# Cosine attention and a low-rank mixer: batch 0's first loads in halves of the heads

## The chip, the cores and the metric

The kernel runs on one core of a Trainium2 chip. Its time is device microseconds of that core, the median of five runs. The engines are TensorE (PE, with its weight loads as PEld), VectorE (DVE), ScalarE (ACT), GpSimd (POOL) and SyncE (SP), which issues most of the DMAs. Each works through its own instructions in order and waits for others by semaphores.

## What is computed

```python
def phi(x, c, s):                       # c, s: cos and sin of pi/2 * position / S
    r = np.maximum(x, 0.0)
    return np.concatenate([r * c, r * s], axis=-1)
q_p, k_p = phi(q, cos_w, sin_w), phi(k, cos_w, sin_w)
kv  = np.einsum('bhsf,bhsd->bhfd', k_p, v)
z   = np.sum(k_p, axis=2)
num = np.einsum('bhsf,bhfd->bhsd', q_p, kv)
den = np.einsum('bhsf,bhf->bhs', q_p, z)[..., None] + 1e-06
x   = (num / den).transpose(0, 2, 1, 3).reshape(B, S, H * D)

h = x.transpose(0, 2, 1) @ U @ V        # mixes positions, rank 32
u = x + h.transpose(0, 2, 1)
out = u + np.maximum(u @ w_ch1, 0.0) @ w_ch2
```

There are 8 batches of 8 heads, 576 positions, 64 columns a head (512 in all), rank 32, and 2048 hidden columns. Inputs and output are float32.

## The kernel before

All 8 batches are processed on the one core. The 576 positions of a batch are five chunks: position 4p + c for p = 0 to 127 is chunk c (0 to 3), and the last 64 positions are the "tail", chunk 4. So q, k and v each come as a main load (`load_main`, 1 MB or half of it, L74) and a tail load (`load_tail`, 128 KB, L80), all issued on SP. The staging buffers of q and v exist once, those of k twice.

The stages of a batch: `q_prep` and `k_prep` (L251, L257) make relu times cosine and relu times sine in bf16, one instruction for each on ScalarE (L237) or VectorE (L239); `v_prep` and `v_block` (L217, L228) cast v, and put a column of ones beside it; `qtr_unit` (L284) transposes q on TensorE with a copy out of PSUM; `kv_unit` (L263) makes kv and z of four heads; `den_unit` (L325) and `recip` the reciprocals of the denominators; `xh_unit` (L341) the normalised x of four heads and one chunk. `A_unit` (L385) is x times U, with an evacuation for each half of the columns; `V_four` and `V_evac` (L196, L207) expand V for all partitions once; `uTd_open`, `uTd_mm` and `uTd_evac` make u transposed for one of four column blocks d, directly in PSUM. `g1_main` (L483) is one of 16 column blocks of the first channel product, four matmuls over d, and its relu goes to ScalarE (L502); `g2_part` (L527) is the second product.

The order on every engine is written out by hand. From L706 on come warm-up matmuls on zeros (`keep_warm`, L176), batch 0's q and k preparation, then `chain_head(0)` and `chain_mid(0)`, and then the first `g1_main`, of which three are opened with two matmuls each because uT of d 0 and 1 is ready first. After that, a list of slots (L775) gives TensorE's dense work, 16 `g1_main` for each batch of a pair, and other work is put beside numbered slots (`at`, `beside`, `PLAN`). Batch 1's preparation lies beside slots 0 to 6, its chain beside slot 7.

Batch 0's loads are issued in the order q, q tail, k, k tail, v tail, v's heads 0 to 3, v's heads 4 to 7, V, U. Then come batch 1's (L722 to L730). U and V are staged in float32 and cast on GpSimd (`cast_uv`, L185). GpSimd also issues the loads of w_ch1, in four quarters that are cast on the way (`w1_load`, L89). It holds the first quarter back by a one-column copy of batch 0's k tail (`mark`, L717), which waits until that tail has landed; the second stands in the middle of `cast_uv`; the third and the fourth wait for batch 1's q tail copy (L755).

Of the kernel before, what the change touches and what calls it, by code (L numbers as in the profile page):

```python
# [10 lines left out]
FP32 = mybir.dt.float32  # L11
BF16 = mybir.dt.bfloat16
# [5 lines left out]
def kernel(  # L18
# [11 lines left out]
    nc = tc.nc  # L30
# [49 lines left out]
    def load_tail(dst, src, b, eng=None):  # L80
        (eng or nc.sync).dma_start(
            out=dst[tail(b), :, :],
            in_=src[b, :, 512:S, :].rearrange("h s d -> s h d"),
        )
# [24 lines left out]
    st_uv = pool.tile([P, 1024], FP32, tag="hid_tl", bufs=1, name="st_uv")  # L109
    stV = st_uv[0:R, 0:S]  # L110
    stU = st_uv[:, S : S + 5 * R].rearrange("p (c r) -> p c r", r=R)

# [8 lines left out]
    for lo in (0, TS):  # L121
# [4 lines left out]
    load_main(qst[0], q, 0)  # L126
    load_tail(qt[0], q, 0)
    load_main(kst[0], k, 0)
    load_tail(kt[0], k, 0)
    load_tail(vt[0], v, 0)  # L130
    load_main(vst[0], v, 0, 0, 4)
    load_main(vst[0], v, 0, 4, 8)
    nc.sync.dma_start(out=stV, in_=moe_V)
    nc.sync.dma_start(
        out=stU[:, 0:4, :], in_=moe_U[0:512, :].rearrange("(p c) r -> p c r", c=4)
    )
    for lo in (0, TS):
        nc.sync.dma_start(out=stU[lo : lo + TS, 4, :], in_=moe_U[512:S, :])
# [23 lines left out]
    V_32 = const.tile([R, 5, P], BF16)  # L162
    V_bf = const.tile([P, 5, P], BF16)
    four = const.tile([R, 4, R], BF16)
    for g in range(4):
        G_.tensor_copy(out=four[:, g, :], in_=ident[0:R, 0:R])
# [14 lines left out]
    V_.memset(U_bf, 0.0)  # L181
    mark = const.tile([TS, 1], FP32)
    mark2 = const.tile([1, 1], FP32)

    def cast_uv():  # L185
        cast(G_, V_32[:, 0:4, :], stV[:, 0:512].rearrange("r (p c) -> r c p", c=4))
        for i in range(2):
            cast(G_, V_32[:, 4, tail(i)], stV[:, 512:S])
        w1_load(1)
        cast(G_, U_bf[:, 0:4, :], stU[:, 0:4, :])  # L190
        for i in range(2):
            cast(G_, U_bf[tail(i), 4 + i, :], stU[tail(i), 4, :])
# [3 lines left out]
    def V_four(tag, bufs):  # L196
        v4 = v4_ps[0] = ps.tile([P, 2, 512], FP32, tag=tag, bufs=bufs, name="v4_ps")
        lhs = four.rearrange("r g s -> r (g s)")
        nc.tensor.matmul(
            out=v4[:, 0, :], lhsT=lhs, rhs=V_32[:, 0:4, :].rearrange("r c t -> r (c t)"),  # L200
            start=True, stop=True,
        )
        nc.tensor.matmul(
            out=v4[:, 1, 0:P], lhsT=lhs, rhs=V_32[:, 4, :], start=True, stop=True
        )
# [135 lines left out]
    def xh_unit(b, c, h0, h1, rec, tag, bufs):  # L341
        x_alloc(b)
        n = h1 - h0
        rows = slice(0, P) if c < 4 else tail(b)
        acc = ps.tile([P, n, D], FP32, tag=tag, bufs=bufs, name="xh_ps")
        for h in range(h0, h1):
            nc.tensor.matmul(  # L347
                out=acc[:, h - h0, :], lhsT=qT_of(b, c, h), rhs=kv_sb[b][:, h, 0:D],
                start=True, stop=True,
            )  # L350
        nc.vector.tensor_tensor(
            out=x_of(b, c, rows)[:, h0 * D : h1 * D].rearrange("p (i d) -> p i d", d=D),
            in0=acc[rows],
            in1=rec[rows, c, :].unsqueeze(2).to_broadcast([P if c < 4 else TS, n, D]),
            op=ALU.mult,
        )
# [214 lines left out]
    def loads(b, eng):  # L571
        def kk():
            alloc_k(b)
            load_tail(kt[b], k, b, eng)
            load_main(kst[b], k, b, eng=eng)

        def vv():
            alloc_v(b)
            load_tail(vt[b], v, b, eng)
            load_main(vst[b], v, b, eng=eng)  # L580

        def qq():
            alloc_q(b)
            load_tail(qt[b], q, b, eng)
            load_main(qst[b], q, b, eng=eng)

        return kk, vv, qq
# [61 lines left out]
    def chain_head(b, fill, xt):  # L649
        if b == 0:  # L650
            v_prep(b, 0, 4, (4,), (A_,))
            v_block(b, 0, 4, 0, 3, V_)
            v_block(b, 0, 4, 3, 4, A_)
        kv_unit(b, 0, "T", 1)
        fill(0)
        rec0 = den_unit(b, 0, 4, "X", 1)
        if b == 0:
            v_prep(b, 4, 8, (4,), (A_,))
        v_block(b, 4, 8, 0, 4, A_)
        fill(1)  # L660
        for n, c in enumerate(ORD):
            xh_unit(b, c, 0, 4, rec0, *xt[n])
            if n == 1:
                fill(2)
            if n == 3:
                kv_unit(b, 1, "T", 1, A_)
        if b == 0:
            V_four("X", 1)
            V_evac(A_)

    def chain_mid(b, fill, xt, dt):
        fill(3)
        m = 3 if b == 0 else 2
        rec1 = den_unit(b, 4, 8, *dt)
        if b == 1:

            nc.sync.dma_start(out=mark2, in_=rec1[0:1, 0, 0:1])
        for n, c in enumerate(ORD[:m]):
            xh_unit(b, c, 4, 8, rec1, *xt[n])
        u01 = ps.tile([P, 2, 512], FP32, tag="X", bufs=1, name="u01")  # L680
        uTd_open(b, 0, None, None, u01[:, 0, :].rearrange("p (c t) -> p c t", c=4))
        uTd_open(b, 1, None, None, u01[:, 1, :].rearrange("p (c t) -> p c t", c=4))
        a0 = A_unit(b, "T", 1, A_, 0, 256)
        for n in (m, m + 1):
            xh_unit(b, ORD[n], 4, 8, rec1, *xt[n])
        fill(4)
        uTd_mm(b, 0)
        uTd_mm(b, 1)
        uTd_evac(b, 0, A_)
        uTd_evac(b, 1, V_ if b == 0 else A_)  # L690
        for n in range(m + 2, 5):
            xh_unit(b, ORD[n], 4, 8, rec1, *xt[n])
        fill(5)
        return a0
# [6 lines left out]
    def warm0(n):  # L701
        m = (2, 1, 0, 1, 1, 2)[n]
        if m:
            keep_warm(m, *(O2 if n == 0 else G3))

    keep_warm(18, "X", 1)  # L706
    for c in TL:
        q_prep(0, c, (V_, V_ if c == 3 else A_))
    for n, c in enumerate(TL):
        qtr_unit(0, c, 0, H, (V_, A_, V_, A_, V_)[n], *(G3 if n < 3 else O2))  # L710
        if n in (1, 3):
            keep_warm(1, "X", 1)
    for c in TL:
        k_prep(0, c, (V_, V_ if c == 3 else A_))
    keep_warm(13, "o", 2)

    G_.tensor_copy(out=mark, in_=kt[0][0:TS, 0, 0:1])  # L717
    w1_load(0)
    cast_uv()
    chain_head(0, warm0, (O2, O2, G3, G3, O2))  # L720
# [10 lines left out]
    a0 = chain_mid(0, warm0, (O2, G3, O2, G3, O2), G3)  # L731
    for c in (0, 1):
        q_prep(1, c, (None, A_))
# [7 lines left out]
    q_prep(1, 0, (V_, None))  # L741
# [7 lines left out]
    for n, c in enumerate(ORD):  # L749
        if n > 1:  # L750
            at(n - 2, lambda c=c, n=n: q_prep(1, c, (V_, (None, A_, V_)[n - 2])))
# [8 lines left out]
    st1 = {}  # L760

# [6 lines left out]
    xt1 = (O2, O2, O2, O2, O2)  # L768
    at(7, lambda: keep_warm(2, "X", 1))
    at(7, lambda: chain_head(1, fill1, xt1))  # L770
    at(7, lambda: st1.update(a=chain_mid(1, fill1, xt1, ("T", 1))))
    at(7, lambda: chain_end(1, st1["a"]))
# [62 lines left out]
```

## Time and profile before

| | us |
|---|---|
| median of 5 runs (319.48 to 321.08) | 320.46 |
| the profiled execution | 320.94 |
| its span, first to last instruction | 319.0 |
| TensorE busy in it | 308.7 |
| first channel product starts | 23.89 |
| batch 1's q tail is on TensorE | 27.21 |
| batch 1's kv starts | 34.63 |

The profile is of one execution. Times in it count from the span's start; the execution's own time has 1.94 us around the span. A row of the timeline has start, duration, engine, line, operation, output and inputs, shape, count, and in brackets how long the engine was idle before it and who ended that. A helper such as `cast` has one line for all its uses, so tiles tell more than lines. The clock granted to TensorE is 1.00 throughout; matmuls of 512 columns follow each other at 0.43 us until 6.2 us, and at 0.22 us from then on.

### The profile page before, as it was taken

Reading aid. Unit: us, or ns where it says so; the run is one execution under the profiler, and the core shown is the slowest. Engines: PE = TensorE matmul, PEld = TensorE weight load, DVE = VectorE, ACT = ScalarE, POOL = GpSimd, SP = SyncE. Lnnn points to the kernel's source line nnn. Section 1 sums busy time; section 2 is a strip of 40 time slices with the busy share of each in tenths; the row PEclk is TensorE's granted clock in tenths of the full one; section 3 lists DMA queues with packets and bytes.
Section 4 is the critical chain, followed back from the end, with each engine's and each line's share of the span. In section 5 each row is a group of like instructions: output and inputs, shape, how many; then the busy total and the mean of one; then the engine's idle time right before and its main releaser. Section 6 shows DMA issues by size and latency. Waiting matters only on the chain.

```text
span 319.0 us, 5754 instructions
## 1 busy us (share of the span) xinstructions
PE 308.7 (97%) x2359; PEld 162.5 (51%) x2386; DVE 154.0 (48%) x341; ACT 150.6 (47%) x251; POOL 35.0 (11%) x71
## 2 busy tenths in 40 slices
PE   8699899999999999999999999999999999999996
PEld 3465464475545544475455444564454444464443
DVE  5767653762877645036926585154836520001211
ACT  3847756685905256658400077559400166650000
POOL 2132500300120140000221100000121100000000
PEclk9999999999999999999999999999999999999999
DMA  7999999999196937990899659930692140001122
GB/s 224 274 284 212 224 206 281 269 277 262 50 202 160 303 90 142 225 276 10 170 206 317 232 121 179 309 104 30 128 214 73 60 91 0 2 0 68 66 83 81
DMA packets 83755, 51.90 MB, mean 163 GB/s; under 512 B 51890, under 2 KB 80946, under 8 KB 83730
## 3 DMA queue, kind: packets, MB, share of 16 engines
q1 hardware_dynamic: 77154, 40.21, 53.4%
q0 software_dynamic: 6432, 11.27, 14.7%
q8 instruction: 18, 0.29, 0.4%
q10 hardware_dynamic: 144, 0.07, 0.1%
q14 instruction: 7, 0.06, 0.1%
HBM read 36.86 MB, written 9.44 MB: 145 GB/s over the span
## 4 chain that ended last, share of the span: by engine, by line
PE 88%; DMA 7%; ACT 3%; DVE 1%; issue 1%; SPq 0%; DVEq 0%; ACTq 0%
PE o_ps L545 39%; PE g_ps L493 33%; PE gt_ps L513 4%; DMA qt<-in_q_dram 4%; DMA kst<-in_k_dram 3%; PE kv_ps L271 3%; PE x_ps L365 3%; PE va_ps L409 3%; ACT k_p L237 1%; PE t_ps L288 1%; PE a_ps L392 1%; ACT hid L502 1%; PE d_ps L330 0%; PE xh_ps L347 0%; ACT k_tl L237 0%
## 5 line engine op out<-in xcount | busy, mean ns | idle before, releaser
L502 ACT ACTIVATE hid<-g_ps 128x512 bf16<-128x512 f32 x128 | 76.2, 596 | 100.0 <-PE g_ps L493 99.4
L493 PE MATMUL g_ps<-uT,w_bf 128*128 128x512 bf16 x512 | 118.5, 379 | 0.2
L545 PE MATMUL o_ps<-w_bf,hid 128*128 128x512 bf16 (+2 forms) x510 | 117.3, 372 | 1.0
L493 PEld LDWEIGHTS <-w_bf 128*128 128x128 bf16 x512 | 48.8, 98 | 55.9 <-issue 0.4
L545 PEld LDWEIGHTS <-hid 128*128 128x128 bf16 x528 | 48.7, 98 | 52.8 <-issue 1.7
L555 DVE TENSOR_TENSOR o_sb<-u_bf,o_ps 128x512 f32<-128x512 bf16 (+2 forms) x33 | 22.1, 668 | 62.7 <-PE o_ps L545 62.6
L565 POOL DMA_DIRECT2D out_dram<-o_sb x24 | 13.5, 562 | 162.9 <-DVE o_sb L555 152.9
L410 DVE TENSOR_TENSOR u_bf<-x_bf,va_ps 128x512 bf16<-128x512 bf16 x32 | 21.8, 685 | 10.2 <-PE va_ps L409 9.7
L105 DVE CAST kv<-kv_ps 128x260 bf16<-128x260 f32 x14 | 6.0, 429 | 32.7 <-PE kv_ps L271 32.7
L237 ACT ACTIVATE q_p<-qst,sinw 128x512 bf16<-128x512 f32 x22 | 15.1, 711 | 4.3 <-DMA qst<-in_q_dram 4.2
L375 DVE TENSOR_TENSOR x_bf<-x_ps,rec 128x512 bf16<-128x512 f32 x24 | 16.6, 691 | 0.8
L513 PE MATMUL gt_ps<-uT_tl,w_bf 128*128 128x128 bf16 x256 | 15.6, 219 | 0.0
L513 PEld LDWEIGHTS <-w_bf 128*128 128x128 bf16 x256 | 14.6, 98 | 0.5
L545 PE MATMUL o_ps<-w_bf,hid_tl 128*128 128x512 bf16 x61 | 14.6, 379 | 0.2
L271 PE MATMUL kv_ps<-v_ext,k_p 128*128 128x65 bf16 x256 | 12.1, 193 | 2.7 <-DVE v_ext L105 1.8
L322 DVE TENSOR_SCALAR rec<-x_ps 128x8 f32<-128x8 f32 (+1 forms) x30 | 4.9, 165 | 20.2 <-PE x_ps L365 20.2
L271 PEld LDWEIGHTS <-k_p 128*128 128x128 bf16 x256 | 11.3, 97 | 6.4 <-ACT v_ext L103 2.0
L409 PE MATMUL va_ps<-A_sb,V_bf 128*128 128x512 bf16 x38 | 14.4, 379 | 0.0
L179 PE MATMUL w_ps<-zero 128*128 128x512 bf16 x38 | 12.1, 456 | 1.9 <-DVE halfpi L142 1.2
L103 ACT ACTIVATE v_ext<-vst 128x512 bf16<-128x512 f32 (+2 forms) x19 | 12.3, 661 | 2.4 <-DMA vst<-in_v_dram 2.3
L239 DVE TENSOR_SCALAR k_p<-kst,cosw 128x512 bf16<-128x512 f32 x27 | 12.8, 493 | 0.9 <-DMA kst<-in_k_dram 0.8
L520 ACT ACTIVATE hid_tl<-gt_ps 128x512 bf16<-128x512 f32 x16 | 9.4, 597 | 5.5 <-PE gt_ps L513 5.5
(105 smaller groups left out, 249.0 us busy)
## 6 DMA issues: line engine op xcount, KB each, us to landing
qst<-in_q_dram SPq DMA_DIRECT2D x8, 1024.0 KB, 10.3
kst<-in_k_dram SPq DMA_DIRECT2D x8, 1024.0 KB, 8.6
vst<-in_v_dram SPq DMA_DIRECT2D x6, 1024.0 KB, 10.4
out_dram<-o_sb POOLq DMA_DIRECT2D x24, 256.0 KB, 3.8
w_bf<-in_moe_w_ch_dram POOLq DMA_DIRECT2D x8, 512.0 KB, 10.4
vst<-in_v_dram SPq DMA_DIRECT2D x4, 512.0 KB, 8.7
out_dram<-o_sb SPq DMA_DIRECT2D x7, 256.0 KB, 2.3
qt<-in_q_dram SPq DMA_DIRECT2D x8, 128.0 KB, 9.5
```

What stands on the lines that cost most here:

```text
L237: nc.scalar.activation(out=o, in_=i, func=AF.Relu, bias=0.0, scale=w)
L239: eng.tensor_scalar(out=o, in0=i, scalar1=0.0, scalar2=w, op0=ALU.max, op1=ALU.mult)
L271: nc.tensor.matmul(out=acc[:, i, :], lhsT=k_p[b][:, c, h, :] if c < 4 else k_tl[:, h, :], rhs=vx[:, c, h, :], start=(c == 0), stop=(c == 4),)
L375: nc.vector.tensor_tensor(out=x_of(b, c, rows).rearrange("p (g i d) -> p g i d", g=2, d=D), in0=view[:, :, :, 0:D], in1=rec[rows].unsqueez ...
L409: nc.tensor.matmul(out=va, lhsT=V_bf[:, c, :], rhs=A_sb[b], start=True, stop=True)
L410: nc.vector.tensor_tensor(out=u_bf[b][:, c, :] if c < 4 else u_tl[b // 2][rows, :], in0=x_of(b, c, rows), in1=va[rows, :], op=ALU.add,)
L493: nc.tensor.matmul(out=g_ps.rearrange("p (c t) -> p c t", c=4), lhsT=w1_bf[:, d, j * P : j * P + P], rhs=uT[b][:, :, d, :], start=(d == 0) ...
L502: nc.scalar.activation(out=hid[b][:, j, :], in_=g_ps, func=AF.Relu, bias=0.0, scale=1.0)
L513: nc.tensor.matmul(out=g_ps[:, jj, :], lhsT=w1_bf[:, d, j * P : j * P + P], rhs=uT_tl[pr][:, d, :], start=(d == 0), stop=(d == 3),)
L545: nc.tensor.matmul(out=o[:, cols], lhsT=lhs[:, j, c * P : c * P + P], rhs=w2_bf[:, j, cols], start=(j == 0), stop=(j == NJ - 1),)
L555: nc.vector.tensor_tensor(out=o_sb[:, cols], in0=u[:, cols], in1=o[:, cols], op=ALU.add)
L565: eng.dma_start(out=out[b, 0:512, cols].rearrange("(p c) n -> p c n", c=4)[:, c, :], in_=o_sb[:, cols],)
```

## The change

Batch 0's q main load is split into two, by heads. k's first half follows it, then the k tail, the q tail, half of the v tail, v's first half, and only then k's second half and the rest of v. The preparations of q and k go by halves as well. V and U come by four casting DMAs that GpSimd issues at the start, without staging; V is expanded from a strided view, on TensorE and VectorE, before the k preparation. GpSimd's `mark` waits for v's first half instead of the k tail, and its cast of v's second half precedes the second `w1_load`. `xh_unit` can normalise on ScalarE, which is used for chunk 1 of heads 0 to 3. The common `chain_head` and `chain_mid` become `chain0` and `chain1`; the latter has the same order of work as before. Of batch 1's q preparation, two early ScalarE instructions move behind the chain, and chunk 0 is done wholly on VectorE. There are fewer warm-up matmuls.

```diff
+    load_main(qst[0], q, 0, 0, 4)
+    load_main(qst[0], q, 0, 4, 8)
+    load_main(kst[0], k, 0, 0, 4)
+    load_tail(kt[0], k, 0)
     load_tail(qt[0], q, 0)
-    load_main(kst[0], k, 0)
-    load_tail(kt[0], k, 0)
-    load_tail(vt[0], v, 0)
+    load_tail(vt[0], v, 0, 0, 4)
     load_main(vst[0], v, 0, 0, 4)
+    load_main(kst[0], k, 0, 4, 8)
+    load_tail(vt[0], v, 0, 4, 8)
     load_main(vst[0], v, 0, 4, 8)
-    nc.sync.dma_start(out=stV, in_=moe_V)
-    ...
+    nc.gpsimd.dma_start(out=V_32, in_=moe_V)
+    nc.gpsimd.dma_start(
+        out=U_bf[:, 0:4, :], in_=moe_U[0:512, :].rearrange("(p c) r -> p c r", c=4)
+    )
+    V_.memset(U_bf[:, 4:6, :], 0.0)
+    for i in range(2):
+        nc.gpsimd.dma_start(out=U_bf[tail(i), 4 + i, :], in_=moe_U[512:S, :])
     for g in range(4):
-        G_.tensor_copy(out=four[:, g, :], in_=ident[0:R, 0:R])
+        V_.tensor_copy(out=four[:, g, :], in_=ident[0:R, 0:R])
...
+        if eng is not None:                                  # in xh_unit
+            for h in range(h0, h1):
+                eng.activation(
+                    out=x_of(b, c, rows)[:, h * D : h * D + D], in_=acc[rows, h - h0, :],
+                    func=AF.Copy, bias=0.0, scale=rec[rows, c, h - h0 : h - h0 + 1],
+                )
+            return
...
+    def chain0():
+        v_prep(0, 0, 4, (4,), (A_,))
+        v_block(0, 0, 4, 0, 3, V_)
+        v_block(0, 0, 4, 3, 4, A_)
+        qtr_unit(0, 4, 0, H, V_, *G3)
+        keep_warm(2, "o", 2)
+        for c in (0, 1):
+            k_prep(0, c, (V_, A_), 4, 8)
+        kv_unit(0, 0, "T", 1)
+        keep_warm(2, "o", 2)
+        for c in (2, 3):
+            k_prep(0, c, (V_, A_), 4, 8)
+        k_prep(0, 4, (A_, A_), 4, 8)
+        rec0 = den_unit(0, 0, 4, "X", 1)
+        v_prep(0, 4, 8, (4,), (G_,))
+        v_block(0, 4, 8, 0, 4, G_)
+        w1_load(1)
+        for n, c in enumerate(TL):
+            xh_unit(0, c, 0, 4, rec0, *(O2, O2, G3, G3, G3)[n], A_ if n == 1 else None)
+        keep_warm(1, "X", 1)
+        kv_unit(0, 1, "T", 1, A_)
+        rec1 = den_unit(0, 4, 8, "X", 1)
+        a0 = A_unit(0, "T", 1, A_, 0, 256)
+        for n, c in enumerate(TL[:3]):
+            xh_unit(0, c, 4, 8, rec1, *(O2, O2, G3)[n])
+        chain_begin(0)
+        uTd_mm(0, 0)
+        uTd_mm(0, 1)
+        for n, c in enumerate(TL[3:]):
+            xh_unit(0, c, 4, 8, rec1, *G3)
+        uTd_evac(0, 0, A_)
+        uTd_evac(0, 1, A_)
+        keep_warm(2, "o", 2)
+        return a0
...
-    keep_warm(18, "X", 1)
+    keep_warm(12, "X", 1)
+    for h in (0, 4):
+        for c in TL[:4]:
+            q_prep(0, c, (V_, V_ if c == 3 else A_), h, h + 4)
+    for c in TL[:4]:
+        qtr_unit(0, c, 0, H, (V_, A_, V_, A_)[c], *(G3 if c < 3 else O2))
+        if c in (1, 3):
+            keep_warm(1, "X", 1)
+    V_four("X", 1)
+    V_evac(V_)
     for c in TL:
-        k_prep(0, c, (V_, V_ if c == 3 else A_))
-    keep_warm(13, "o", 2)
-    G_.tensor_copy(out=mark, in_=kt[0][0:TS, 0, 0:1])
+        k_prep(0, c, (V_, A_ if c < 3 else V_), 0, 4)
+    q_prep(0, 4, (V_, A_))
+    keep_warm(10, "o", 2)
+    G_.tensor_copy(out=mark, in_=vst[0][0:TS, 0, 0, 0:1])
     w1_load(0)
-    cast_uv()
-    chain_head(0, warm0, (O2, O2, G3, G3, O2))
+    a0 = chain0()
...
-    for c in (0, 1):
-        q_prep(1, c, (None, A_))
     chain_end(0, a0)
...
-    q_prep(1, 0, (V_, None))
+    q_prep(1, 0, (V_, V_))
...
-            at(n - 2, lambda c=c, n=n: q_prep(1, c, (V_, (None, A_, V_)[n - 2])))
+            at(n - 2, lambda c=c, n=n: q_prep(1, c, (V_, A_ if n % 2 == 0 else V_)))
```

## The prediction

> **What bounds the kernel now.** I read the page's busy shares first, then the stages, the chain that ended last, and TensorE's and GpSimd's instructions in order of time around the change.
>
> ```profile
> PE 308.7 (97%) x2359; PEld 162.5 (51%) x2386; DVE 154.0 (48%) x341; ACT 150.6 (47%) x251; POOL 35.0 (11%) x71
> ```
>
> TensorE is nearly always busy, but its first 24 us are mostly warm-up matmuls and short attention products. The table by stage (stretch, length, busy time and instructions of PE, PEld, DVE, ACT, POOL; clock, DMA share, GB/s):
>
> ```profile
> 6.20:14.00 7.80, 7.09 (x61) 4.33 (x61) 6.41 (x15) 6.70 (x10) 1.09 (x2) 1.00 1.12 286
> 14.00:15.70 1.70, 0.00 (x0) 0.00 (x0) 0.70 (x2) 1.11 (x4) 0.44 (x1) 1.00 0.89 222
> 15.70:24.00 8.30, 7.93 (x156) 5.60 (x158) 5.61 (x17) 4.06 (x8) 2.85 (x7) 1.00 1.15 287
> 24.00:26.70 2.70, 2.66 (x12) 0.94 (x11) 1.18 (x3) 1.43 (x3) 0.00 (x0) 1.00 1.19 238
> 26.70:27.20 0.50, 0.00 (x0) 0.00 (x0) 0.47 (x2) 0.48 (x2) 0.00 (x0) 1.00 1.15 241
> 34.40:37.20 2.80, 1.55 (x22) 0.92 (x22) 1.16 (x4) 2.03 (x4) 2.69 (x4) 1.00 1.21 231
> 37.20:319.00 281.80, 277.29 (x2036) 144.44 (x2058) 128.18 (x277) 126.86 (x212) 22.38 (x40) 1.00 0.64 152
> ```
>
> DMA is saturated from 6 to 37 us (share about 1). From 37.2 us on, 277.29 of 281.80 us are TensorE work that the change leaves alone. So the change is worth what it moves the dense work that starts at 24 us. The chain (start, length, what) says what places that:
>
> ```profile
> 2.05 9.60 DMA kst<-in_k_dram
> ...
> 11.67 1.95 ACT k_p L237 x3
> ...
> 13.72 12.69 DMA qt<-in_q_dram
> ...
> 26.44 0.72 ACT q_tl L237
> ...
> 27.21 0.62 PE t_ps L288 x8
> ```
>
> It does not run through batch 0's chain at all, but through batch 1's q tail, a load in a full queue. TensorE's rows in order of time agree:
>
> ```profile
> 23.89 0.61 PE L493 MATMUL g_ps<-uT,w_bf 128*128 128x512 bf16 x2
> 24.34 0.59 PE L458 MATMUL uT_ps<-V_bf,A_sb 128*128 128x512 bf16 x2
> 24.77 1.89 PE L493 MATMUL g_ps<-uT,w_bf 128*128 128x512 bf16 x8
> 27.21 0.62 PE L288 MATMUL t_ps<-ident,q_tl 128*128 128x128 bf16 x8 [0.56 <-ACT q_tl L237]
> ```
>
> The first channel-mixing product starts at 23.89; 12 matmuls later TensorE waits 0.56 us for the tail. And the first product has two conditions: batch 0's last copy of d 0, 1 (VectorE, done 23.90), and the first quarter of w_ch1. GpSimd's rows, and the issue in its window (KB, us to landing):
>
> ```profile
> 12.91 0.47 POOL L717 COPY mark<-kt 64x1 f32<-64x1 f32 x1 [10.34 <-DMA kt<-in_k_dram]
> 13.33 1.11 POOL L91 DMA_DIRECT2D w_bf<-in_moe_w_ch_dram  x1
> ...
> 18.36 0.78 POOL L91 DMA_DIRECT2D w_bf<-in_moe_w_ch_dram  x1
> ```
>
> ```profile
> w_bf<-in_moe_w_ch_dram POOLq DMA_DIRECT2D x1, 512.0 KB, 10.5
> ```
>
> 13.33 + 10.5 = 23.83: the weight lands as the chain ends. So **three things tie** at 24 to 27 us: chain, w_ch1, q tail. Call T the landing of w_ch1's first quarter: the transposes can start at T + (26.66 - 23.83) = T + 2.83, or at the q tail's landing + 0.77, and T below 24.38 costs nothing.
>
> **The change part by part.**
>
> *q0 in halves.* 1 MB lands at 6.6; at the 379 to 387 GB/s of the 3 to 5 us slices half a megabyte is 1.4 us, so the first half is there at about 5.2, when VectorE ends its memsets (4.81, plus four small copies that it takes over from GpSimd, where they took 0.64). The five VectorE operations of 0.478 become ten, taken as 0.26 (half and a little); ScalarE's three of 0.706 become six of 0.42 (the 128x256 cast's row). Five of either precede the second half's arrival. q's prep ends near 7.9 (now 8.68), its transposed copies near 9.7 (now 10.98). Worth nothing alone: the k prep waits for k until 11.67.
>
> *Order of the queue; k0 in halves.* First half of v now stands behind 1 MB of q, half of k, the k and q tails and half a v tail. Measured steps in this queue: tails 0.8 to 1.3 us (kt0 landed 12.9, vt0 13.7), half-megabytes 1.4 (15.1, 16.5). From kt0's 12.9, v's first half has the same large pieces ahead or in it, one half tail more (0.5), and the U, V pieces from the other queue (0.3 to 0.5): 13.7. From its old 15.1: less half of k (1.4), less half a tail (0.5), plus U, V: 13.6. The two agree: **v's first half about 1.4 us sooner**, k's second half about 15, v's second half 16.5 + 0.5 = 17.0. The kv product of heads 0 to 3 starts near 14.3 instead of 15.74, but its evacuation stands on VectorE behind two cosine preps of k's second half, which now wait for it: done about 16.1 against 16.98. Reciprocal and normalisation follow that much sooner.
>
> *v's second cast on GpSimd*, 1.20 us by the 128x1024 row there, ScalarE now 1.08, and begun at 17.0 instead of 16.53: heads 4 to 7 of kv start near 18.3 (now 18.20). So the 0.9 us won on heads 0 to 3 goes into waiting there. Behind that cast on GpSimd waits the second w_ch1 load: 18.3 to 18.4, now 18.36. Nil.
>
> *U and V by casting DMA.* SP loses four issues (9.71 to 12.93), so batch 1's q is issued sooner; no gain, since the queue ahead of it is full and its bytes don't shrink. GpSimd loses 1.46 + 0.72 of casts. V's expansion and copy leave the middle of the chain (TensorE 0.38 + 0.21, ScalarE 0.70), and go before the k prep on VectorE: 640 elements by the 0.69 of 512 are 0.86. The strided read of V costs between 0.38 and four times that, inside the wait for k. If V lands by 10 this is covered; if later, up to 13, it eats the 0.9 above first.
>
> *One normalisation on ScalarE*: four activations of 64 columns. From 0.39 for 256 and 0.60 for 512, 0.23 each: 0.93 on ScalarE for 0.35 on VectorE. Covered by the wait for v's second half.
>
> *Tail of the chain.* From kv of heads 4 to 7 at 18.3: 0.6 + copy 0.39 + denominators 0.64 + reciprocal 0.5 + five normalisations 0.35 to 0.42 = 22.4, then A's second half and copy; the two uT copies (0.60 each, both on ScalarE) end near 23.0 to 23.4 (now 23.90, where the second one, on VectorE, waited 0.55 for the first). **Chain: 0.5 to 0.9 sooner.**
>
> *The first w_ch1 load* is now released by v's first half (13.7) instead of kt0 (12.91): **0.8 later**. Against it: this is now GpSimd's first DMA, with 1.11 for the issue where the second took 0.78, and nothing of its queue moving before 17.5 (the queues' view of 14.5 to 17.5 lists the hardware queue alone). If that is the price of a first use, U and V pay it, and 0.3 to 1.3 comes back. T lies between 22.9 and 24.6; I take **24.6**, since the later loads on this queue also took 8 to 10 us. Cost 24.6 - 24.38 = 0.2.
>
> *The q tail* has the same bytes before it. A w_ch1 load 0.8 later leaves fewer weight pieces interleaved ahead: landing 25.6 to 26.4. It doesn't bind if T is 24.6.
>
> *Batch 1's preps.* Two ScalarE preps at 23.25 (1.33) go from a time when it idles into 26.4 to 31, less the one of chunk 2: net one 0.70 more there. ScalarE idles 0.71 before 30.92, so 0 at best and 0.7 at worst in kv of batch 1, whose wait is on ScalarE (0.53 and 0.41). I take 0. VectorE gets one 0.44 more; its k prep ends 35.09 against ScalarE's 35.95, so it is covered. Weights 2 and 3 start after the q tail's copy, 0.4 later, with 0.8 in hand.
>
> *Warm-up.* 38 dummies become 29 or so, all before 24 us. Here a rule speaks against the change: the Trainium skill (TensorE: Matmul & The Clock Gate, What's actually happening) halves the clock after an idle window of about 3.4 us. The row 14.00:15.70 has 1.70 us idle, and the matmuls after it still follow at 0.22, cold ones at 0.43. By the row nothing is lost: my longest new gap is 1 to 1.5 us. By the rule, if V comes after 12.5, the gap from 9 on is long enough, and the clock could be half when the dense work starts: 3.4 us at half rate, 1.7 lost.
>
> *More, smaller loads.* The Trainium skill (DMA: Bandwidth & Descriptors, Rules for kernel authors) wants 1 MB and more per transfer, and its Anatomy of one DMA puts about 2.0 us fixed on each. By the rule, three more transfers could be 6 us; the row of v's halves says 1.4 us from landing to landing at the rate of a full queue, so about 0. I take the row.
>
> **Sum.** Span 319.0 + 0.2; around it 320.94 - 319.0 = 1.94: 321.14. The profiled execution is 0.48 above the median of the runs, so 320.66, **320.7**.
>
> **The rivals.** *A, the tie holds* (0.40): as summed, 320.0 to 321.4. *B, the weight comes late* (0.27, slower): w_ch1 waits for a v half that is hardly sooner than now, say at 15.1 (+2.2): T = 26.0, loss 1.6, 322.1. It decides from T = 25.35. For it: every load here ends late by what is interleaved; the release is one position further back. Against: two counts give 13.7. *C, all three ends move* (0.25, faster): first use already paid, T = 22.9, chain 23.2, q tail 25.4: transposes at 26.2, 1.0 sooner, 319.4. Against: batch 1's k lands at about 31 and its prep starts at 31.54, so 0.4 is kept unless that moves too. *D, cold clock* (0.08): 0.2 + 1.7, 322.4. That the halves do nothing at all is inside A.
>
> **How the numbers follow.** 0.3% of 320.46 is 0.96, about what a measurement tells from no change: within 319.5 to 321.4 is A but for 0.07 at its ends (0.02 faster, 0.05 slower), so same 0.33; faster 0.25 + 0.02 = 0.27; slower 0.27 + 0.08 + 0.05 = 0.40. Range 318.9 to 322.8: C's and B's middles with the 0.5 that their landings are uncertain by; A alone 320.0 to 321.4.
>
> **What would show it.** Right: heads 0 to 3's kv at about 14.3, GpSimd's cast of v ending near 18.3, first g product waiting for w_ch1 at about 24.6, transposes of the q tail at 27.2 to 27.5. Wrong: v's first half after 14.5; g waiting on a uT copy; matmuls at 0.43 after 24; kv of batch 1 starting more than 0.5 from 34.6.

## The result

The changed kernel takes 0.9959 of the time of the kernel before (95% interval 0.9945 to 0.9972): medians 320.09 us (44 runs) and 321.27 us (79 runs). That is 0.41% or 1.2 to 1.3 us less, just over the 0.3% that a measurement can tell. The forecast was "the same", 320.7 us against 320.46; the direction is that of case C, which had a chance of 0.25. That 320.7 lies only 0.6 from 320.09 is luck: the five runs that it started from were 0.8 faster than the 79, and the forecast added 0.2 where 1.2 to 1.3 went away.

The profiled execution of the changed kernel has a span of 318.4 us and a time of 320.13 us. First the page's row of engines, then the table by stage (stretch, length, busy time and instructions of PE, PEld, DVE, ACT, POOL; clock, DMA share, GB/s):

```profile
PE 308.0 (97%) x2352; PEld 162.2 (51%) x2378; DVE 155.5 (49%) x355; ACT 150.7 (47%) x260; POOL 36.6 (12%) x67
```

```profile
6.20:14.00 7.80, 5.70 (x55) 3.55 (x56) 6.94 (x21) 5.68 (x12) 1.91 (x2) 1.00 1.16 299
14.00:15.70 1.70, 1.61 (x28) 0.98 (x25) 1.43 (x5) 1.70 (x5) 1.17 (x3) 1.00 1.09 389
15.70:24.00 8.30, 7.66 (x138) 5.29 (x139) 6.21 (x18) 3.83 (x12) 1.19 (x2) 1.00 1.17 254
24.00:26.70 2.70, 2.70 (x26) 1.75 (x25) 2.67 (x8) 2.65 (x5) 0.44 (x2) 1.00 1.16 290
34.40:37.20 2.80, 2.50 (x30) 1.30 (x29) 1.44 (x4) 0.64 (x2) 0.04 (x1) 0.69 1.24 207
37.20:319.00 281.80, 276.59 (x2012) 143.67 (x2032) 127.16 (x274) 125.77 (x211) 22.39 (x40) 1.00 0.56 149
```

Two rows matter most. In 14.00:15.70 TensorE works, where it stood still, and the queues move 389 GB/s where they moved 222. In 34.40:37.20 the granted clock is 0.69, so a stretch at half clock lies in it. TensorE's rows in order of time:

```profile
22.27 0.59 PE L491 MATMUL g_ps<-uT,w_bf 128*128 128x512 bf16 x2
22.71 0.59 PE L456 MATMUL uT_ps<-V_bf,A_sb 128*128 128x512 bf16 x2
23.14 1.89 PE L491 MATMUL g_ps<-uT,w_bf 128*128 128x512 bf16 x8
24.86 0.61 PE L279 MATMUL t_ps<-ident,q_tl 128*128 128x128 bf16 x8
...
33.03 0.20 PE L262 MATMUL kv_ps<-v_ext,k_p 128*128 128x65 bf16 x1 [0.53 <-ACT k_p L228]
33.65 0.20 PE L262 MATMUL kv_ps<-v_ext,k_p 128*128 128x65 bf16 x1 [0.41 <-ACT k_p L228]
...
35.35 1.81 PE L491 MATMUL g_ps<-uT,w_bf 128*128 128x512 bf16 x4
...
39.95 1.02 PE L491 MATMUL g_ps<-uT,w_bf 128*128 128x512 bf16 x4
```

The first channel product is 1.62 us sooner (23.89 before), the q tail's transposes 2.35 (27.21), and the bracket in which TensorE waited 0.56 us for that tail is gone. Batch 1's kv starts at 32.28 (34.63), also 2.35 sooner, with the same waits of 0.53 and 0.41 inside. Then four matmuls take 1.81 us, where four take 1.02 at full clock (the last row): the record of the clock shows half from 35.5 to 38.9, which costs some 1.6 us. 2.35 less 1.6 and small changes is the 0.7 by which this span is shorter.

The chain that ended last (start, length, what) now leaves a load at 10.9 and runs through batch 0's own chain, whose last copies of d 0 and 1 are the ScalarE row below it:

```profile
3.15 7.71 DMA qt<-in_q_dram
...
15.65 0.93 DVE k_p L230 x2
...
17.07 0.93 ACT x_bf L344 x4
18.00 0.29 ACT kv L103
...
21.89 0.55 PE uT_ps L442 x8
22.44 0.43 PE g_ps L491 x2
...
25.03 0.45 PE t_ps L279 x8
```

```profile
20.69 1.08 ACT L103 ACTIVATE uT<-u 128x512 bf16<-128x512 f32 x2 [0.97 <-PE u L456]
```

Its DMA is batch 0's q tail, no longer batch 1's; the copies end at 21.77, and the first product does not wait for the weight. GpSimd's rows, and the weight's issue (KB, us to landing):

```profile
12.09 0.18 POOL L738 COPY mark<-vst 64x1 f32<-64x1 f32 x1 [7.85 <-DMA vst<-in_v_dram]
12.21 1.96 POOL L91 DMA_DIRECT2D w_bf<-in_moe_w_ch_dram  x1
...
15.11 1.06 POOL L105 CAST v_ext<-vst 128x1024 bf16<-128x1024 f32 x1 [0.53 <-DMA vst<-in_v_dram]
16.12 0.77 POOL L91 DMA_DIRECT2D w_bf<-in_moe_w_ch_dram  x1
```

```profile
w_bf<-in_moe_w_ch_dram POOLq DMA_DIRECT2D x1, 512.0 KB, 9.0
```

v's first half is there at 12.1 (forecast 13.7), its second half is cast from 15.11 (forecast 17.0), and w_ch1 lands at 12.2 + 9.0 = 21.2 (forecast 24.6). These came 1.6 to 3.4 us sooner than the sum had them.

### The profile page after: what moved, and what is told of

It reads as the page before. It is cut to its first block, busy times and chain, and to the rows that moved or that the text cites. A ratio compares the mean times of both kernels' runs of the same rounds, so it can differ in the third digit from the quotient of the medians.

```text
span 318.4 us, 5764 instructions
## 1 busy us (share of the span) xinstructions
PE 308.0 (97%) x2352; PEld 162.2 (51%) x2378; DVE 155.5 (49%) x355; ACT 150.7 (47%) x260; POOL 36.6 (12%) x67
## 4 chain that ended last, share of the span: by engine, by line
PE 89%; ACT 4%; DMA 2%; DVE 2%; issue 1%; SPq 1%; DVEq 0%; ACTq 0%
PE o_ps L543 39%; PE g_ps L491 33%; PE gt_ps L511 4%; PE kv_ps L262 3%; PE x_ps L363 3%; PE va_ps L407 3%; DMA qt<-in_q_dram 2%; ACT hid L500 2%; PE a_ps L390 1%; PE t_ps L279 1%; ACT k_p L228 1%; ACT q_p L228 1%; DVE k_p L230 1%; PE xh_ps L338 1%; PE d_ps L321 1%
## 5 line engine op out<-in xcount | busy, mean ns | idle before, releaser
L491 PE MATMUL g_ps<-uT,w_bf 128*128 128x512 bf16 x512 | 120.0, 382 | 0.1
L105 DVE CAST kv<-kv_ps 128x260 bf16<-128x260 f32 x14 | 6.0, 429 | 32.2 <-PE kv_ps L262 32.1
L228 ACT ACTIVATE q_p<-qst,sinw 128x512 bf16<-128x512 f32 (+1 forms) x24 | 15.1, 658 | 2.2 <-DMA qst<-in_q_dram 2.2
L313 DVE TENSOR_SCALAR rec<-x_ps 128x8 f32<-128x8 f32 (+1 forms) x30 | 4.9, 165 | 20.3 <-PE x_ps L363 20.2
L230 DVE TENSOR_SCALAR k_p<-kst,cosw 128x512 bf16<-128x512 f32 (+1 forms) x31 | 13.9, 469 | 0.0
L262 PE MATMUL kv_ps<-v_ext,k_p 128*128 128x65 bf16 x256 | 12.2, 193 | 0.9 <-ACT k_p L228 0.9
L363 PEld LDWEIGHTS <-q_pT 128*128 128x128 bf16 x192 | 9.1, 98 | 5.5 <-issue 0.6
L230 DVE TENSOR_SCALAR q_p<-qst,cosw 128x512 bf16<-128x512 f32 (+1 forms) x28 | 11.6, 435 | 0.1
```

The costliest lines, as they stand in the source:

```text
L228: nc.scalar.activation(out=o, in_=i, func=AF.Relu, bias=0.0, scale=w)
L230: eng.tensor_scalar(out=o, in0=i, scalar1=0.0, scalar2=w, op0=ALU.max, op1=ALU.mult)
L262: nc.tensor.matmul(out=acc[:, i, :], lhsT=k_p[b][:, c, h, :] if c < 4 else k_tl[:, h, :], rhs=vx[:, c, h, :], start=(c == 0), stop=(c == 4),)
L363: nc.tensor.matmul(out=acc[:, g, i * E : i * E + E], lhsT=qT_of(b, c, h), rhs=kv_sb[b][:, h, :], start=True, stop=True,)
L491: nc.tensor.matmul(out=g_ps.rearrange("p (c t) -> p c t", c=4), lhsT=w1_bf[:, d, j * P : j * P + P], rhs=uT[b][:, :, d, :], start=(d == 0) ...
```

## The experiments

**What could be behind it.** *Theory Q*: SP. In the traces SP's loads use eight completion semaphores in turn (a semaphore is the counter that tells that a load has landed), and a load is issued only when the eighth before it has landed, whatever their buffers: in the kernel before, k's main load of batch 1 goes at 15.12 after v's first half landed at 15.10, its tail at 16.52 after 16.50, and batch 1's q at 13.06 after the k tail landed at 12.86. There, the view of SP's waits shows loads of batch 1's k waiting for batch 0's v, with which they share no buffer:

```profile
SPq L75 <- DMA vst<-in_v_dram: 0.5, 1, 0.5
SPq L81 <- DMA vst<-in_v_dram: 0.5, 1, 0.5
```

SP's own rows, before:

```profile
7.98 1.68 SPq L75 DMA_DIRECT2D vst<-in_v_dram  x1
9.71 1.57 SPq L133 DMA_DIRECT2D st_uv<-in_moe_V_dram  x1
11.32 0.42 SPq L134 DMA_DIRECT2D st_uv<-in_moe_U_dram  x1
11.79 1.14 SPq L138 DMA_DIRECT2D st_uv<-in_moe_U_dram  x2
13.06 0.50 SPq L75 DMA_DIRECT2D qst<-in_q_dram  x1
```

and after:

```profile
9.10 0.60 SPq L75 DMA_DIRECT2D vst<-in_v_dram  x1
9.83 0.42 SPq L75 DMA_DIRECT2D qst<-in_q_dram  x1
```

With V and U gone from SP, batch 1's q is issued 3.2 us sooner. Its rivals: *the chain* (the halves, v's cast, V's expansion and the normalisation end batch 0's chain sooner, and U and V are only along), *the weight* (what counts is when w_ch1 is released), *the clock* (fewer stretches at half clock), and *chance* (one profiled execution against another).

**Both kernels again**, for the spread.

> The kernel before, unchanged, for a second trace on the chip of the three runs beside it. In its first trace the loads landed late: q at 6.6 us where the changed kernel's whole q was there by 5.6, though nothing differs up to then. Theory 1 (the change moves the loads): a second trace of the kernel before looks like the first, first channel product at 23.9, q tail of batch 1 transposed at 27.2, and the ratio is 1.000 +- 0.003. Theory 2 (how fast the loads go differs from execution to execution, and the two traces happened to differ): q lands near 5.6 here too, the first product starts 1 us or more sooner than 23.9, and much of the 2.35 us between the two traces at the q tail's transposes is not the change's.

> The changed kernel, unchanged, on the same chip. Theory 1: first product at 22.3, transposes of the q tail at 24.9, again 2.3 sooner than the kernel before; ratio 0.995 to 0.997. Theory 2: it stands only 0.5 to 1.2 us ahead of the kernel before's trace from the same chip at these two places. Either way: where the granted clock is 0.995 and not 1.000, the matmuls after batch 1's first kv are at 0.43 us for some 3.4 us and the run is about 1.6 us longer.

> The changed kernel, unchanged, beside the two runs above: ratio 0.9950 to 0.9970; transposes at 24.8 to 25.4, kv of batch 1 at 32.2 to 32.9, batch 1's q issued at 9.8 to 10.7.

The kernel before against itself: 0.999 (0.9969 to 1.001). The changed one: 0.997 (0.9943 to 0.9997) and 0.9961 (0.9929 to 0.9993). The profiles scatter: the q tail's transposes start at 27.21 and 26.40 before, at 24.86, 25.27 and 25.20 after. A fourth profile of the changed kernel (a0_fourth, below) has them at 26.97, with a half-clock stretch from 20.1 on. So the 2.35 us above is the largest difference that these profiles give; the two nearest without half clock ahead of them are 1.1 apart. Span less the cost of the half-clock stretches is 319.0 and about 319.2 before, 316.8, 317.4, 317.1 and 317.5 after.

**The halves alone**: into the kernel before.

```diff
-    load_main(qst[0], q, 0)
+    load_main(qst[0], q, 0, 0, 4)
+    load_main(qst[0], q, 0, 4, 8)
-    load_main(kst[0], k, 0)
+    load_main(kst[0], k, 0, 0, 4)
+    load_main(kst[0], k, 0, 4, 8)
```

> The kernel before; only q's and k's main loads of batch 0 are each issued as two half-megabyte loads, in the same order, with the preparation left whole. In both traces of the kernel before, the last piece of each load of batch 0 comes 1 to 2.5 us after the rest (k is used at 11.7 and 12.2), in the two traces of the changed kernel it does not. Theory H (the 1 MB loads cause that lag, the halves cure it): q used at 5.6 to 5.9 in place of 6.6, k at 10 to 10.5, v at 13 to 13.7, first product 0.5 to 1 sooner, ratio 0.997 to 0.999. Theory O (the order and the whole new head do it, not the size of a load): q at 6.5 to 6.7, k at 11.5 to 12.2, first product at 23.1 to 23.9, ratio 1.000.

1.0015 (0.9978 to 1.0052): nothing that can be told, neither a gain nor a price for two loads more. Only the loads are split here; the preparations by halves, which go with them in the changed kernel, are not in it.

**U and V by casting DMA alone**: into the kernel before, with the second `w1_load` released by v's second half; once more on another chip; with that second load held until v's second half is cast; and, without any casting DMA, V and U only moved up on SP, to right behind q.

```diff
-    nc.sync.dma_start(out=stV, in_=moe_V)
-    ...
+    nc.gpsimd.dma_start(out=V_32, in_=moe_V)
+    ...
-    cast_uv()
+    G_.tensor_copy(out=mark, in_=vst[0][0:TS, 4, 0, 0:1])
+    w1_load(1)
```

> The kernel before with U and V by casting DMA from GpSimd at the start, without staging and casts; V is still expanded after kv of heads 4 to 7. The second w_ch1 load is released when v's second half has landed. Theory U (four loads fewer on SP and the casting queue's first use moved to the start are what helps): the first w_ch1 quarter lands 1 us or more sooner than 23.8, its first packets 2 us after its issue and not 3.2; batch 1's q lands 1 us sooner; first product 23.4 to 23.9, bound by the chain, q tail's transposes at 26.2 to 26.6, ratio 0.997 to 0.999. Theory O: landings within 0.5 of the kernel before's, ratio 0.999 to 1.001.

> U and V by casting DMA in the kernel before, as in the first run of it, again with five rounds. It had 0.9983 with an interval that holds both none and all of the gain. Theory Q: 0.9970 to 0.9985, a little over half of the changed kernel's on the same chip; transposes at 25.4 to 26.0, kv of batch 1 at 32.8 to 33.6. If the head's order and halves do the rest: 0.999 or more.

> The kernel before with U and V by casting DMA as in the run above, but with the second w_ch1 load held until v's second half has been cast (about 17.5), near where the kernel before issues it. That run had released it at 15.5. Theory Q: the earlier second weight is not what helped: batch 1's q is issued at 9.5, first product at 22.8 to 23.2, transposes at 25.4 to 26, kv of batch 1 by 33.3, ratio 0.997 to 0.9985. Rival (it was the second weight): transposes stay at 25.6, but slot 4 waits for the weight and kv of batch 1 is back at 34 to 34.6, ratio 0.999 to 1.001.

> The kernel before; only the four loads of V and U stand second to fifth on SP, behind q, and no longer ahead of batch 1's q. Queue, bytes, staging and casts are unchanged. Theory Q (the place among SP's loads decides, since each waits for the eighth before it: batch 1's q waited for the k tail's landing at 12.86): batch 1's q is issued at 10 to 11, lands at 19 to 20, its tail at 22 to 23.5, w_ch1 at 22 to 22.5, transposes at 25.5 to 26, kv of batch 1 at 33 to 33.7, ratio 0.997 to 0.999. Rival (the casting queue's own pace is what helped): batch 1's q is issued early too, but lands at 22 to 23 and the tail at 25 to 26.5, transposes at 26.4 to 27.2, ratio 0.999 to 1.002.

Measured: 0.9983 (0.9958 to 1.0008), 0.9984 (0.9959 to 1.0009), 0.9996 (0.9968 to 1.0024) and 0.9996 (0.9966 to 1.0026). Taken together, the first two are 0.9984 with a half-width of 0.0025 / 1.41 = 0.0018: at most a part of the gain, and not told from none. In b_uv_ahead nothing changes but the place of these loads on SP, and it shows no gain either. Yet the traces do what theory Q says: batch 1's q is issued at 9.54 to 9.93 in all four, and in b_uv the transposes start at 25.56. Its row of the stage where the queues differed:

```profile
14.00:15.70 1.70, 1.08 (x22) 0.80 (x22) 0.85 (x3) 1.66 (x4) 0.38 (x2) 1.00 1.08 386
```

386 GB/s where the kernel before had 222. Over the profiles of all kernels run, that stretch moved 209 to 298 GB/s where q was issued at 12.2 or later, and 319 to 389 where it was issued at 11.2 or sooner, with one exception in fourteen (258 at 10.57).

**The order of the loads, and what releases w_ch1.** The changed kernel with the old order (halves kept); the same with `mark` on the k tail again; the changed order with `mark` on the k tail.

```diff
     load_main(kst[0], k, 0, 0, 4)
+    load_main(kst[0], k, 0, 4, 8)
     load_tail(kt[0], k, 0)
     load_tail(vt[0], v, 0, 0, 4)
-    load_main(vst[0], v, 0, 0, 4)
-    load_main(kst[0], k, 0, 4, 8)
     load_tail(vt[0], v, 0, 4, 8)
+    load_main(vst[0], v, 0, 0, 4)
     load_main(vst[0], v, 0, 4, 8)
...
-    G_.tensor_copy(out=mark, in_=vst[0][0:TS, 0, 0, 0:1])
+    G_.tensor_copy(out=mark, in_=kt[0][0:TS, 0, 0:1])    # a_order_mark, a_mark
```

> The changed kernel with its halves, but in the old order: q, q tail, k in both halves, k tail, v tails, v in both halves. Theory O (the order is worth most): v's first half comes 1.5 to 2 later than 12.1, kv of heads 0 to 3 at 15.5 to 16, the w_ch1 load is issued at 14 and lands at 23 to 24, first product at 23 to 24, the gain of 1.3 us is gone: ratio 0.999 to 1.002. Theory H (halves alone): only k's preparation for all heads is there sooner, v's second half, which ends the chain, keeps its place: first product at 22.3 to 22.9, ratio 0.996 to 0.998.

> The changed kernel with batch 0's loads in the old order (halves kept) and the first w_ch1 load released by the k tail and not by v's first half. The run with the old order alone had v's first half at 14.61, the weight issued at 15.18 and landed at 25.81, the first product at 25.86. If that loss of 3 us was the release: the weight is issued at 13.1 to 13.4, lands at 23 to 24, first product at 23 to 24, ratio 0.998 to 1.001. If it was the order of the data itself: first product stays at 25 or later and the ratio at 1.004 and more.

> The changed kernel with the first w_ch1 load released by the k tail, as before the change, in place of v's first half. The k tail is there about 2.5 to 3 us sooner, so the load is issued at about 9.3 in place of 12.2. My forecast's step (the landing of w_ch1 binds the first product, and its later release costs time): first product 0.5 to 1.5 sooner than 22.3 to 22.7, ratio 0.991 to 0.995. Theory O (the chain binds at 22.3): w_ch1 lands at 18 to 19 and nobody waits for it; v's and k's second halves come 0.5 to 1 later because the weight takes turns with them, so the first product is at 22.8 to 23.5 and the ratio is 0.997 to 1.000.

1.006 (1.0025 to 1.0095), 0.9956 (0.9927 to 0.9985) and 0.9946 (0.9908 to 0.9984). TensorE in a_order:

```profile
25.86 0.61 PE L491 MATMUL g_ps<-uT,w_bf 128*128 128x512 bf16 x2 [1.26 <-DMA w_bf<-in_moe_w_ch_dram]
...
28.46 0.61 PE L279 MATMUL t_ps<-ident,q_tl 128*128 128x128 bf16 x8
```

and in a_order_mark:

```profile
22.97 0.59 PE L491 MATMUL g_ps<-uT,w_bf 128*128 128x512 bf16 x2
...
25.56 0.61 PE L279 MATMUL t_ps<-ident,q_tl 128*128 128x128 bf16 x8
```

This is rival B, shown: with v's first half in its old place, w_ch1 is released at 15.18 instead of 13.03, lands at 25.81 instead of 21.62, and the kernel takes about 1%, some 3.3 us, longer than a_order_mark. Beside the kernel before it loses 322.87 - 321.12 = 1.75 us. Released by the k tail, the old order is as good as the new one. So the new order of q, k and v is worth nothing that can be told by itself; it makes the new condition of `mark` harmless.

**U and V back on SP.** a_uvsp is the changed kernel with the four loads on SP, casts on GpSimd, and V expanded behind heads 4 to 7 of kv. It differs in two things, the loads with their casts and V's place in the chain; a_dead has the loads alone. It is the changed kernel, casting DMAs and all, plus the four loads on SP into a buffer that nobody reads. a0_fourth is the changed kernel on the same chip.

```diff
     load_main(vst[0], v, 0, 4, 8)
+    nc.sync.dma_start(out=stV, in_=moe_V)
+    nc.sync.dma_start(
+        out=stU[:, 0:4, :], in_=moe_U[0:512, :].rearrange("(p c) r -> p c r", c=4)
+    )
+    for lo in (0, TS):
+        nc.sync.dma_start(out=stU[lo : lo + TS, 4, :], in_=moe_U[512:S, :])
...
+        cast(G_, V_32, stV)             # a_uvsp alone, as are those of U, in chain0
```

> The changed kernel with its order and halves, but U and V as before: four float32 loads on SP behind v, casts on GpSimd, V expanded behind kv of heads 4 to 7. Theory Q (what counts is when SP issues batch 1's q: it was held to 13.06 by the issues of V and U and by kt0's landing at 12.86, and goes at 9.8 to 10.6 in the changed kernel, so q has landed before w_ch1's packets start at 16.3): q is issued at 12.5 to 13.2 again, lands at 21 to 23 in place of 17.7 to 19.2, w_ch1 at 22 to 23, the q tail at 23 to 25, transposes at 25.7 to 26.5, kv of batch 1 at 33.5 to 34.5; ratio 0.998 to 1.000, a loss of 0.7 to 1.2 us on the changed kernel. Theory O (the order of batch 0's loads is what counts): first product by 23.0, transposes by 25.5, ratio 0.996 to 0.997.

> The changed kernel with four loads added on SP behind v's second half, of V and U into a buffer that nobody reads: what the casting DMAs took off SP is put back, and nothing else. Theory Q (the place of batch 1's q on SP is what moved the head): batch 1's q is issued at 12.5 to 13.0 instead of 9.8 to 10.6, the stretch of 14.0 to 15.7 us falls from 340 to 389 GB/s to under 300, batch 1's k tail lands after 30, the first product waits for the weight or the transposes of the q tail for it, and the ratio is 0.998 to 1.000. The rival (the gain is batch 0's chain, and U and V are only along): the loads cost their 144 KB, 0.4 us at 350 GB/s, in a queue that has time to spare, and the ratio stays at 0.995 to 0.9975.

> The changed kernel as it is, beside the run with the four loads put back: 0.9945 to 0.9972 as before; it is there so that the two stand on one chip.

0.9976 (0.9942 to 1.001), 0.9959 (0.9937 to 0.9981) and 0.9941 (0.9919 to 0.9964). The first can be told neither from the kernel before nor from the changed one. In a_dead's trace theory Q does all that it announced, and more. SP, then TensorE's waits:

```profile
12.43 1.14 SPq L141 DMA_DIRECT2D st_uv<-in_moe_U_dram  x2
13.70 0.50 SPq L75 DMA_DIRECT2D qst<-in_q_dram  x1
```

```profile
24.38 0.61 PE L501 MATMUL g_ps<-uT,w_bf 128*128 128x512 bf16 x2 [1.46 <-DMA w_bf<-in_moe_w_ch_dram]
29.90 1.03 PE L289 MATMUL t_ps<-ident,q_tl 128*128 128x128 bf16 x8 [2.76 <-ACT q_tl L238]
```

The queues move 241 GB/s in 14.00:15.70, batch 1's k tail lands at 32.55, and the span is 323.4. But that profiled execution took 325.19 us, the longest of 13, and their median is 320.15: the ratio lies where the rival put it (0.995 to 0.9975), not at 0.998 to 1.000. **Theory Q fails as the explanation of the whole gain.** The mechanism is there in the trace and can be costly in one execution; in the median, putting the four loads back costs 320.15 - 319.51 = 0.64 us beside a0_fourth, with intervals that overlap, of the 321.81 - 319.51 = 2.30 that a0_fourth gains there. So a part of about a quarter is neither shown nor excluded. The changed kernel without SP's relief is still faster than the kernel before.

**The clock.** Six more warm-up matmuls just before batch 1's kv (`at(7, ...)`), behind which the half-clock stretches begin.

```diff
-    at(7, lambda: keep_warm(2, "X", 1))
+    at(7, lambda: keep_warm(8, "X", 1))
```

> The changed kernel with 8 warm-up matmuls ahead of batch 1's chain in place of 2. TensorE waits there for k's preparation (0.53 and 0.41 us in the changed kernel's trace) and then for kv's evacuation, so six more of 0.216 = 1.3 us, of which 0.9 to 1.1 fill the wait. Theory C (the low activity around that wait halves the clock for one window in some executions): all runs at clock 1.000, and the mean is 0.3 to 0.8 us lower than the changed kernel's, ratio 0.992 to 0.995. Rival (the half clock has nothing to do with that wait): the share of runs at 0.995 stays, and the time rises by 0.2 to 0.4 us.

> The kernel before with the same 8 warm-up matmuls for 2 at the same place. Theory C: if the kernel before has the half clock in some executions as well, it gains 0.2 to 0.6 us; if never, it loses 0.2 to 0.4 (1.3 us of matmuls against 0.94 us of waits there). Ratio 0.998 to 1.001.

0.9961 (0.9943 to 0.9979) for the changed kernel and 0.9987 (0.9968 to 1.0007) for the one before, beside 0.997 and 0.999 without it on the same chip. Both ratios move by under 0.001. The executions whose mean clock is 0.9985 or more say the same: beside one another, the kernel before and the changed one average 320.80 and 319.65 us (36 and 8 executions), 320.95 and 319.36 (27 and 9), 321.28 and 319.22 (12 and 7). The clock isn't what sets the two kernels apart.

**Versions that might beat both.** a_best: `mark` on the k tail, and the sine of batch 1's chunk 3 of k on VectorE instead of ScalarE. a_mark_warm: `mark` on the k tail, and eight warm-ups.

```diff
-        at((4, 5, 5, 6, 6)[n], lambda c=c, n=n: k_prep(1, c, (V_, A_)))
+        at((4, 5, 5, 6, 6)[n], lambda c=c, n=n: k_prep(1, c, (V_, V_ if n == 4 else A_)))
```

> A candidate to beat both: the changed kernel, first w_ch1 load released by the k tail, and batch 1's last sine preparation of k (chunk 3) on VectorE in place of ScalarE. In the changed kernel's trace kv of batch 1 waits for ScalarE at 33.03 and 33.65 while VectorE has been idle since 32.44. One ScalarE preparation of 0.66 less, one VectorE preparation of 0.44 more (ending at 32.9): kv's wait shrinks from 0.94 to 0.3 to 0.4. Expected: kv of batch 1 done 0.5 to 0.6 sooner against its own start, ratio 0.993 to 0.995. If something else binds there (kv's evacuation, v's cast), no gain over the changed kernel: 0.995 to 0.997.

> The changed kernel with the first w_ch1 load released by the k tail and 8 warm-up matmuls ahead of batch 1's chain in place of 2. Of 22 runs with the 8 in the changed kernel 2 had a half-clock window, of 54 without 16. If that holds: at most 2 of some 14 runs below clock 0.9985, mean 0.3 to 0.5 lower than the changed kernel's on this chip, ratio 0.993 to 0.996. If the share is a third again: the 8 matmuls do nothing there and cost 0.2 to 0.4, ratio 0.996 to 0.998.

a_best: 0.9963 (0.9931 to 0.9994), no more than the change. a_mark_warm: 0.9933 (0.991 to 0.9956), faster than the kernel before and the lowest ratio of all; beside the changed kernel on the same chip (0.9961) it isn't told apart.

## Why the prediction was wrong

**What bounds the kernel** was read rightly: the tie at 24 to 27 us sets the end, and the 281.80 us behind it keep their work (276.59 us of TensorE now, 277.29 before).

**Where it failed** is the arrival of batch 0's data, and through it T. The steps "*v's second half 16.5 + 0.5 = 17.0*", "*k's second half about 15*" and "*v's first half about 1.4 us sooner*" took the landings of the trace before and shifted them by bytes, at the rate of "a full queue". The queue wasn't full. The DMA share of about 1 hid that: the summary lines of 10 to 14 us, before and then after, are

```profile
DMA packets 1274, 1.08 MB, mean 271 GB/s; under 512 B 293, under 2 KB 1258, under 8 KB 1274
```

```profile
DMA packets 1611, 1.39 MB, mean 348 GB/s; under 512 B 317, under 2 KB 1611, under 8 KB 1611
```

with shares of 114.4% and 109.5%: the engines count as no less busy while they move a fifth less. So in the profiled execution k's second half landed at 13.7, v's first at 12.0 and its second at 15.1, 1.3 to 1.9 us sooner than summed (v's first half at 12.4 to 13.2 in the three other profiles of the changed kernel, k's second at 14.0 to 14.5, v's second at 15.5 to 16.7). From 10 to 14 us the four profiles of the changed kernel moved 348, 336, 337 and 290 GB/s, the two of the kernel before 271 and 237. Why this queue moves more is only half settled: where q of batch 1 is issued sooner the next stretch is fuller, in thirteen of fourteen profiles; why 10 to 14 us differ already isn't shown.

**T = 24.6** was the late end of 22.9 to 24.6: a release 0.8 later, and the same 10.5 us from there to the landing. The weight landed at 21.24, 22.62, 21.28 and 23.84 in four profiles of the changed kernel: the release at 12.2 to 13.9, so on average no later than the 13.33 before, and 8.7 to 10.0 us from issue to landing instead of 10.5. The latest of the four is still 0.8 sooner than the value taken. Nor does it bind: in a_mark the weight is released at 11.07 and lands at 21.3, and the first product starts at 22.96 without a wait; only in a0_again does the product wait for the weight, for 0.19 us.

```profile
22.96 0.59 PE L491 MATMUL g_ps<-uT,w_bf 128*128 128x512 bf16 x2
```

The argument for C, a first use of the casting queue that U and V pay ("*0.3 to 1.3 comes back*"), was the better one in size. In the first two profiles it doesn't show: w_ch1's first packet moves 4.1 us after its issue in the changed kernel and 4.3 before. Over all twenty it moves 2.9 to 4.4 us after the issue in the fourteen where U and V went by that queue ahead of it, 3.8 on average, and 4.2 to 5.3 in the other six, 4.7 on average. That the first use is the reason isn't shown.

**The chain, "0.5 to 0.9 sooner"**, had its mechanism right and its size wrong. Heads 0 to 3 of kv start at 14.41 (forecast 14.3), V's copy took 0.82 (0.86), GpSimd's cast of v 1.06 (1.20), the four ScalarE normalisations 0.93 (0.93). But that cast ends at 16.17 and not 18.3 (16.5 to 17.8 in the three other profiles), since v's second half was there, and "the 0.9 us won on heads 0 to 3 goes into waiting there" did not happen. The two uT copies end at 21.77, 2.1 us sooner than before (21.81, 22.12 and, behind a half-clock stretch, 23.57 in the others).

**"U and V by casting DMA ... no gain, since the queue ahead of it is full and its bytes don't shrink"**: wrong in the trace, as theory Q's rows show, and hardly wrong in time: alone 0.9984 ± 0.0018, and a_dead keeps most of the gain without the relief of SP. **The q tail, "25.6 to 26.4"**, landed at 21.5 to 24.8, before the transposes could have used it.

**The cap of C, "0.4 is kept unless that moves too"**: it moved. Batch 1's k tail landed at 28.4 to 30.8 in the four profiles of the changed kernel, where it had landed at 31.1 and 32.2. From the transposes to batch 1's kv TensorE has 7.42 us of work; it took 7.42 before, 8.94 in b0_again, where k was late, and 7.42 to 7.73 after. Moving ScalarE's two preps behind the chain cost nothing there, as taken.

**More, smaller loads.** The row was the better guide: b_half's two loads more cost nothing that can be told (1.0015, 0.9978 to 1.0052), where "*about 2.0 us fixed on each*" would have been 4 us, or 1.0125. That figure is one for loads that GpSimd issues; these go by SP.

**The rivals.** B is a true mechanism, and sized well: in a_order the weight lands at 25.81 (26.0 forecast), and the loss against the kernel before is 1.75 us (1.6 forecast). D happened as an event and not as a difference. The Trainium skill (TensorE: Matmul & The Clock Gate, What's actually happening) ties half clock to an idle window of about 3.4 us; the trace shows it after 3.43 us in which TensorE was busy for 2.19 us with small matmuls:

```profile
32.06:35.49 3.43, 2.19 (x43) 1.51 (x43) 1.40 (x3) 2.98 (x5) 2.38 (x4) 0.99 1.24 208
```

The same stretch in a0_third is as busy, and no half clock follows it:

```profile
32.40:35.83 3.43, 2.19 (x43) 1.52 (x43) 1.88 (x4) 2.97 (x5) 2.12 (x3) 1.00 1.24 207
```

It also fell in b0_again, from 37.5 to 44.3, so both kernels pay it.

**What stays open.** The gain is shown, and so is that no single outer part carries it: halves 1.0015, order nothing, U and V 0.9984, U and V put back 0.9959 to 0.9976. What is left is batch 0's chain as rewritten (the preparations by halves, v's cast on GpSimd, V's expansion ahead of k, the ScalarE normalisation, fewer warm-ups, batch 1's q later), and parts that are each too small to be told alone. That it is this is argued by exclusion; none of these was run alone.

## What to carry to other kernels

A DMA share of 1 is no proof of a full queue: read the GB/s beside it, stretch by stretch, and the row of issues, before moving landings about by their bytes. Where a term has two ends and three others hang on it, as T here, the middle is safer than the end that makes the change worthless. And a mechanism that one trace shows at 2 us can be worth 0.6 or less in the median: put it back alone, and time it.

## What the hardware showed that was not expected

The same queue moved 222 to 389 GB/s in the same stretch of 1.7 us, depending on what had been issued.

A stretch at half clock of 3.4 us (6.8 in b0_again) came behind 3.4 us in which TensorE was busy for 2.19 us in the changed kernel and for 1.55 in b0_again; in a0_again 1.99 us of 3.43 at the same place brought none. So how busy that stretch was doesn't tell whether half clock follows. In a_warm8 and a0_fourth it came at 20.1 to 20.2 instead, inside batch 0's chain, behind 1.88 and 2.29 us of 3.41. A mean clock under 0.9985 shows in 59 of 176 executions of the kernel before that stood beside the experiments, in 22 of 76 of the changed one, and in 6 of 47 with eight warm-ups; the medians hardly see it.

VectorE's cosine of a chunk of k, 0.48 us each, took longer beside GpSimd's cast of v; in a_best these are VectorE's row and GpSimd's:

```profile
30.35 1.76 DVE L230 TENSOR_SCALAR k_p<-kst,cosw 128x512 bf16<-128x512 f32 x2
```

```profile
30.78 1.04 POOL L105 CAST v_ext<-vst 128x1024 bf16<-128x1024 f32 x1 [0.39 <-DMA vst<-in_v_dram]
```

Two of them took 1.76 us, and 1.72 and 1.67 beside the same cast in a0_again and a0_third. In a_best the sine moved to VectorE comes behind them, and batch 1's kv waits 0.55 us for ScalarE and 0.64 for VectorE, where it waited 0.53 and 0.41 for ScalarE: what was taken off ScalarE did not end that preparation any sooner.
